# All four head pairs of a 256-token unit in one batch of array tiles per level, TensorE in program order, v through DRAM, first step of 512 tokens

## The chip, the cores and the metric

One core of one Trainium2 chip runs the kernel. The metric is device microseconds of that core, median of three runs. The profile is one further execution taken by the hardware profiler. Engines are named as in the profile: PE is TensorE's matmul, PEld its weight load, DVE VectorE, ACT ScalarE, POOL GpSimd, SP the queue that issues the DMAs.

## What is computed

A gated linear recurrence per head (batch 4, 8 heads, 768 tokens, head size 48), then a feed-forward layer on the 3072 tokens of width 8 x 48 = 384, inner width 2048, with a quick GELU:

```
f = 1 / (1 + exp(-f_logit))
state = 0
for t in range(S):
    state = f[:, :, t, :, None] * state + einsum('bhd,bhe->bhde', k[:, :, t], v[:, :, t])
    y[:, :, t] = einsum('bhd,bhde->bhe', q[:, :, t], state)
x = y.transpose(0, 2, 1, 3).reshape(B * S, H * D)
h = x @ w_in
out = (h * (1 / (1 + exp(-1.702 * h)))) @ w_out
```

All inputs are 32-bit floats but the two weight matrices, which arrive as 64-bit floats; the kernel turns their bits into 32-bit floats itself.

## The kernel before

**Units and pairs.** The 3072 tokens are 12 units of 256 tokens (`U`), three in each batch entry. A unit's heads are worked off as four pairs (`a`), two heads stacked on the 128 partitions, one in rows 0 to 47, the other in rows 64 to 111 (`rows`). `attention(n, a, ...)` does one pair: it turns f_logit, q and k with six transposes on TensorE (L187, L192), makes `F` (sigmoid, ACT, L188), `X` (q, q times f, k; L193, L194) and products of f over 2, 4, ... 64 tokens (`tot`, POOL, L203). In a chunk of 64 tokens the recurrence is replaced by six levels (`LEV` = 1, 2, 4, ... 32). At each level, tokens of the second halves meet keys of the first halves: four small matmuls give scores into `sc` (L217), one for each head and each group of 128 tokens (48 rows by 64 columns of the array each). Between two levels `promote` (L331, DVE) multiplies half of q and k in place by products of f, and ACT copies the keys of the next level to `Kc` (L235). DVE moves scores from PSUM to `A` under a mask, four slots of 64 at a time (L241). `add` multiplies `A` with rows of v (`vl`, seven arrangements of v, one for each level and half) into `py` (L256). Then k is turned back (L274, `kn`), gives the state increment of each chunk (`pd`, L281), the states follow each other in `st` (L293, L296), and q times f meets the state before its chunk in `py` (L306). ACT copies `py` to `yT` (L315), and ten DMAs in a unit (L320) carry it to `xT`, the input of the feed-forward layer, 0.5 us each to issue.

**Feed-forward.** `mlp_step` runs on a step: the first of unit 0 alone (256 tokens), five of two units (512 tokens) and the last of unit 11. It makes 16 blocks of h (three matmuls each, L342; sigmoid on ACT, L346; product on DVE, L347) and then, for each 128 tokens, 16 matmuls of 384 columns into `po` (L352). A 32-bit matmul shows as two instructions of each kind in the profile.

**Order.** The program text puts the attention of the next step between pieces of this step's feed-forward. The scheduler of the framework then orders every engine by itself; two lists of order edges (`issue_after`, L174) keep the matmuls on the banks of `py` apart. So on TensorE the bursts of small matmuls of one pair stand one by one between feed-forward matmuls.

**Loads.** `load_unit` issues six loads of raw q, k, f_logit, two of v by token (`vn`) and 28 of `vl`, whose pieces are single heads' rows of 48 floats. `raw`, `ld` and `att` tiles have two buffers, `sc`, `tr` and `y` in PSUM one. The weights (`load_weights`, L109) come in 28 pieces after unit 0, each with six DVE operations (L127 to L134) and one on POOL (L135).

## Time and profile before

| | us |
|---|---|
| median of three runs | 965.14 (960.77 to 965.42) |
| the profiled execution's own time | 966.6 |
| its span, first to last instruction | 964.9 |
| PE busy in it | 879.1 |

A row of the chain of waits gives a start and the time from there to the next piece of the chain, all in us; a row of a group gives total busy us and the mean ns of one. Busy time of PE is not work done, since ends of matmuls are modelled; how long a run of matmuls takes is read from when the next one starts. The granted clock (PEclk) has two levels, 1.2 GHz (0.50) and 2.4 GHz (1.00). No clock is recorded before 75 us, and the page shows 1.00 there.

### The profile page before, as it was taken

The page shows a single profiled execution, that of the slowest core. Times are in us where ns is not written, and L with a number is a line of the kernel's source. Part 1 is how long each engine was busy: PE and PEld are TensorE (multiplying, and loading weights), DVE is VectorE, ACT ScalarE, POOL GpSimd, SP SyncE. Part 2 cuts the span into 40 slices and gives each one's busy share as a digit, 9 for nine tenths or more (in the row PEclk, how much of TensorE's full clock was granted, in tenths as well). Part 3 has the DMA queues.
Part 4 walks back from the last instruction along what each step waited for, and adds up shares of the span by engine and source line. Part 5 has one row for each costly group of instructions (what it writes and reads, how often), then busy time and mean ns, then how long its engine had stood idle before and what let it go on. Part 6 is the DMA issues. An engine that isn't in the chain of part 4 may idle for free.

```text
span 964.9 us, 20905 instructions
## 1 busy us (share of the span) xinstructions
PE 879.1 (91%) x8672; PEld 473.7 (49%) x8672; DVE 385.3 (40%) x904; ACT 240.8 (25%) x617; POOL 126.0 (13%) x345
## 2 busy tenths in 40 slices
PE   2677888667799999999999999999999999999998
PEld 1444644343444555444555444555444554445584
DVE  1688866332344323344332444322444233331220
ACT  1212211222233222233222333222333222221120
POOL 5233323101001011010010100101001010000000
PEclk9997987655699999999999999999999999999999
DMA  7743363161442613314314315205206100000000
GB/s 113 180 133 102 113 161 98 44 99 22 65 67 42 99 33 70 71 29 55 64 42 69 69 21 81 59 20 110 39 12 108 35 26 14 5 5 13 22 9 16
DMA packets 205343, 58.78 MB, mean 61 GB/s; under 512 B 193985, under 2 KB 201665, under 8 KB 205249
## 3 DMA queue, kind: packets, MB, share of 16 engines
q1 hardware_dynamic: 205248, 57.45, 29.7%
q8 instruction: 68, 1.11, 0.5%
q14 instruction: 27, 0.21, 0.1%
HBM read 47.97 MB, written 4.72 MB: 55 GB/s over the span
## 4 chain that ended last, share of the span: by engine, by line
PE 83%; DVE 7%; SPq 3%; ACT 3%; POOL 2%; issue 2%; DMA 1%; DVEq 0%; ACTq 0%
PE o L352 28%; PE h L342 27%; PE sc L217 9%; PE y L256 7%; PE y L306 3%; PE tqk L192 3%; PE dS L281 2%; PE tk L274 2%; PE tf L187 2%; DVE X L331 2%; POOL w_out L135 1%; SPq L163 1%; DVE A L241 1%; DVE s L131 1%; DVE a L134 1%
## 5 line engine op out<-in xcount | busy, mean ns | idle before, releaser
L352 PE MATMUL o<-w_out,g 128*128 128x384 f32 x768 | 306.0, 517 | 8.7 <-POOL w_out L135 8.7
L342 PE MATMUL h<-xT,w_in 128*128 128x512 f32 (+1 forms) x672 | 307.7, 571 | 0.8 <-DMA xT<-yT 0.6
L352 PEld LDWEIGHTS o<-w_out,g 128*128 128x128 f32 x768 | 131.2, 193 | 67.4 <-POOL w_out L135 10.5
L331 DVE TENSOR_TENSOR X<-X,tot 128x256 f32<-128x256 f32 x240 | 105.1, 438 | 131.3 <-PE sc L217 130.9
L235 ACT COPY Kc<-X 128x128 f32<-128x128 f32 x240 | 71.8, 299 | 295.6 <-DVE X L331 295.6
L342 PEld LDWEIGHTS h<-xT,w_in 128*128 128x128 f32 x672 | 113.5, 194 | 38.2 <-issue 21.4
L217 PEld LDWEIGHTS sc<-X,Kc 48*64 48x64 f32 x1920 | 58.0, 143 | 142.8 <-ACT Kc L235 135.2
L217 PE MATMUL sc<-X,Kc 48*64 48x64 f32 x1920 | 93.0, 258 | 27.1 <-ACT Kc L235 26.9
L256 PEld LDWEIGHTS y<-A,vl 64*48 64x48 f32 x2688 | 70.6, 133 | 75.2 <-DVE A L241 45.6
L203 POOL TENSOR_TENSOR tot<-F 128x128 f32<-128x128 f32 x48 | 19.6, 409 | 665.7 <-ACT F L188 665.6
L256 PE MATMUL y<-A,vl 64*48 64x64 f32 (+1 forms) x2688 | 91.1, 251 | 14.6 <-DVE A L241 14.1
L347 DVE TENSOR_TENSOR g<-h,sg 128x512 f32<-128x512 f32 (+1 forms) x112 | 68.4, 612 | 86.4 <-ACT sg L346 86.4
L241 DVE TENSOR_TENSOR A<-sc,masks 128x512 f32<-128x512 f32 x96 | 66.4, 691 | 74.5 <-PE sc L217 74.5
L346 ACT ACTIVATE sg<-h 128x512 f32<-128x512 f32 (+1 forms) x112 | 60.0, 536 | 102.6 <-PE h L342 97.5
L296 DVE SCALAR_TENSOR_TENSOR st<-st,tot,dS 128x48 f32<-128x48 f32 x176 | 46.5, 264 | 66.6 <-PE dS L281 61.1
L194 DVE TENSOR_TENSOR X<-X,F 128x256 f32<-128x256 f32 x48 | 20.4, 425 | 122.5 <-ACT X L193 122.4
L203 POOL TENSOR_TENSOR tot<-tot 128x64 f32<-128x64 f32 (+4 forms) x240 | 63.4, 264 | 18.6
L315 ACT COPY yT<-y 48x256 f32<-48x256 f32 x96 | 35.1, 366 | 78.4 <-PE y L306 77.2
L306 PEld LDWEIGHTS y<-X,st 48*48 48x48 f32 x704 | 27.1, 130 | 39.8 <-DVE st L296 28.2
L276 ACT COPY kn<-tk 128x256 f32<-128x256 f32 x48 | 17.9, 372 | 105.7 <-PE tk L274 105.7
L217 PEld LDWEIGHTS sc<-X 48*64 48x64 f32 x768 | 24.2, 150 | 38.1 <-DVE X L194 37.6
L217 PE MATMUL sc<-X 48*64 48x128 f32 (+1 forms) x768 | 31.3, 282 | 12.1 <-DVE X L194 11.6
(33 smaller groups left out, 421.5 us busy)
## 6 DMA issues: line engine op xcount, KB each, us to landing
bits<-in_moe_w_in_dram SPq DMA_DIRECT2D x12, 512.0 KB, 3.5
bits<-in_moe_w_out_dram SPq DMA_DIRECT2D x16, 384.0 KB, 3.3
raw<-in_f_logit_dram SPq DMA_DIRECT2D x24, 192.0 KB, 3.2
raw<-in_q_dram SPq DMA_DIRECT2D x24, 192.0 KB, 4.6
raw<-in_k_dram SPq DMA_DIRECT2D x24, 192.0 KB, 5.0
vn<-in_v_dram SPq DMA_DIRECT2D x24, 192.0 KB, 3.1
vl<-in_v_dram SPq DMA_DIRECT2D x24, 192.0 KB, 3.3
vl<-in_v_dram SPq DMA_DIRECT2D x96, 48.0 KB, 2.4
```

Source lines behind the costliest of these rows:

```text
L203: nc.gpsimd.tensor_tensor(tn, t2[:, :, 0], t2[:, :, 1], ALU.mult)
L217: nc.tensor.matmul(sc[g * HS:(g + 1) * HS, h, slot * 64:slot * 64 + w], lhsT=lhs(h, g), rhs=rhs(h, g), start=True, stop=True,)
L235: nc.scalar.copy(Kc[:, l, :].rearrange("p (n m) -> p n m", m=LEV[l]), X[:, 2].rearrange("p (n two m) -> p n two m", two=2, m=LEV[l])[:, :, ...
L241: nc.vector.tensor_tensor(At, sc[:, :, :256].rearrange("p h (s t) -> p h s t", t=64), masks[r].unsqueeze(1).broadcast_to((P, 2, 4, 64)), A ...
L256: prior.append(nc.tensor.matmul(dst(h, g), lhsT=vl[g * 64:(g + 1) * 64, u, 2 * a + h, :], rhs=rhs(h, g), start=start, stop=False, skip_gro ...
L296: nc.vector.scalar_tensor_tensor(st[:, c, :], before, D64[:, c:c + 1], d, op0=ALU.mult, op1=ALU.add)
L306: mm = nc.tensor.matmul(py[rows(h), c // 2, c % 2 * C:(c % 2 + 1) * C], lhsT=before[rows(h)], rhs=X[rows(h), 1, c * C:(c + 1) * C], start= ...
L331: nc.vector.tensor_tensor(qk, qk, by, ALU.mult)
L342: nc.tensor.matmul(ph, lhsT=w_in[:, n, ff * P:(ff + 1) * P], rhs=xT[:, n, :T], start=(n == 0), stop=(n == NK - 1))
L346: nc.scalar.activation(sg, ph, AF.Sigmoid, scale=1.702)
L347: nc.vector.tensor_tensor(g[-1][:, ff % FG, :], ph, sg, ALU.mult)
L352: nc.tensor.matmul(po, lhsT=g[ff // FG][:, ff % FG, tt * P:(tt + 1) * P], rhs=w_out[:, ff, :], start=(ff == 0), stop=(ff == NFF - 1),)
```

## The change

TensorE keeps the order of the program text (`manual_schedule`); the other engines are still ordered by the scheduler. `attention(n, ...)` now makes a list of 16 parts for a whole unit, with all four pairs in each: six T parts (four transposes each, j = f, q, k by two pairs), a W part with the first scores of level 1, a W part with the rest of them, level 2 and the first `add`, four W parts for the levels 4 to 32 (scores of one level, `add` of the one before), two T parts that turn k back, a W part with the last `add` and the state increments, and a W part with q against the states and the way out. The matmuls are the same in number and shape. `F`, `X`, `tot`, `Kc`, `A` hold 1024 columns in place of 256, so each DVE, ACT and POOL operation of a level does four pairs at once; `promote` of a level is issued ahead of the move of its scores (`evacuate`). The state's one operation for a chunk and pair becomes two for a chunk.

`merge` puts feed-forward blocks (`mlp_h`: one h block, `mlp_o`: four matmuls of one output tile) behind the parts, 16 blocks to a unit, three shares for a W part and one for a T part: behind the 16 parts stand 1, 0, 1, 0, 1, 0, 2, 1, 2, 1, 2, 1, 1, 0, 2, 1 blocks. The steps are six of 512 tokens. Step 0's h blocks run in two halves of 256 tokens in units 1 and 2, its outputs in unit 3; then step s runs in units 2s + 2 and 2s + 3, and step 5 alone at the end.

v goes to a buffer in DRAM in token order by one DMA, and from there to `vl` in seven DMAs with rows of 1536 bytes and to `vn` in one, issued behind the fifteenth part of the unit before. `raw`, `ld` and `att` have one buffer, but `yT`, `st`, `A` and `Kc` keep two. The weights come in 56 smaller pieces in units 0 to 2, each with two ACT operations (Sign, Abs), four on DVE and two on POOL.

```diff
-    ld = ctx.enter_context(tc.tile_pool(name="ld", bufs=2))
-    att = ctx.enter_context(tc.tile_pool(name="att", bufs=2))
+    ld = ctx.enter_context(tc.tile_pool(name="ld", bufs=1))
+    att = ctx.enter_context(tc.tile_pool(name="att", bufs=1))
+    ctx.enter_context(tc.manual_schedule(engines={mybir.EngineType.PE}))
...
-    raws = [const.tile([P, 3, NG, H, HS], F32, name=f"raw{j}") for j in range(2)]
-    for t in raws:
-        nc.gpsimd.memset(t[:, :, :, :, D:], 0.0)
+    raw = const.tile([P, 3, NG, H, HS], F32, name="raw")
+    for j in range(3):
+        nc.vector.memset(raw[:, j, :, :, D:], 0.0)
...
+    v_toks = [tc.dram_tile([U, DM], F32, name=f"v_tok{j}") for j in range(2)]
+    WI, WO = 256, 192
...
-        bits = wp.tile([P, w, 2], I32, tag="bits", name=f"bits_{n}")
+        nc.sync.dma_start(out=bits.rearrange("p c two -> p (c two)"), in_=src.bitcast(I32))
...
-        a, s = tmp("a"), tmp("s")
-        ve.tensor_scalar(a, hi, 0x7FFFFFFF, None, op0=ALU.bitwise_and)
-        ve.tensor_scalar(s, hi, -(1 << 31), -(1 << 31), op0=ALU.bitwise_and, op1=ALU.bitwise_xor)
-        af = a.bitcast(F32)
-        ve.tensor_scalar(af, af, 2.0 ** 112, 2.0 ** 97, op0=ALU.mult, op1=ALU.max)
-        ve.scalar_tensor_tensor(s, a, 3, s, op0=ALU.logical_shift_left, op1=ALU.bitwise_xor)
-        ve.tensor_scalar(a, s, -(1 << 23), None, op0=ALU.bitwise_and)
-        ve.scalar_tensor_tensor(af, lo.bitcast(U32), 2.0 ** -52, af, op0=ALU.mult, op1=ALU.mult)
-        po.tensor_tensor(dst, s.bitcast(F32), af, ALU.add)
+        nc.scalar.activation(sign, hi.bitcast(F32), AF.Sign)
+        nc.scalar.activation(a, hi.bitcast(F32), AF.Abs, scale=2.0 ** 112)
+        ve.tensor_scalar(a, a, 2.0 ** 97, None, op0=ALU.max)
+        ve.tensor_scalar(
+            s.bitcast(I32), a.bitcast(I32), 3, -(1 << 31), op0=ALU.logical_shift_left, op1=ALU.bitwise_xor
+        )
+        ve.tensor_scalar(a.bitcast(I32), s.bitcast(I32), -(1 << 23), None, op0=ALU.bitwise_and)
+        ve.scalar_tensor_tensor(a, lo.bitcast(U32), 2.0 ** -52, a, op0=ALU.mult, op1=ALU.mult)
+        po.tensor_tensor(a, a, s, ALU.add)
+        po.tensor_tensor(dst, a, sign, ALU.mult)
...
-        for u, (m, half) in enumerate(V_HALF):
-            src = v[b, :, s0:s0 + U, :].rearrange("h (n two m) d -> two n m h d", two=2, m=m)[half]
-            nb = U // (2 * m)
-            if m <= nb:
-                for i in range(m):
-                    nc.sync.dma_start(out=vl[i:P:m, u], in_=src[:, i])
-            else:
-                for i in range(nb):
-                    nc.sync.dma_start(out=vl[i * m:(i + 1) * m, u], in_=src[i])
+    def load_v(n):
+        b, s0 = n // NU, n % NU * U
+        v_tok = v_toks[n % 2]
+        nc.sync.dma_start(
+            out=v_tok.rearrange("t (h d) -> t h d", h=H),
+            in_=v[b, :, s0:s0 + U, :].rearrange("h t d -> t h d"),
+        )
+        vl = ld.tile([P, NV, DM], F32, tag="vl", name=f"vl_{n}")
+        for u, (m, half) in enumerate(V_HALF):
+            nc.sync.dma_start(
+                out=vl[:, u], in_=v_tok.rearrange("(n two m) e -> two n m e", two=2, m=m)[half]
+            )
+        vn = ld.tile([P, NG, DM], F32, tag="vn", name=f"vn_{n}")
+        nc.sync.dma_start(out=vn, in_=v_tok.rearrange("(g p) e -> p g e", g=NG))
+        return vl, vn
...
+    TILES = [(h, g) for h in range(2) for g in range(NG)]
...
+            pt = ps.tile([P, 2, NG, P], F32, tag="tr", name=f"t{'fqk'[j]}_{n}_{a0}")
+            for a in range(2):
+                for g in range(NG):
+                    nc.tensor.transpose(
+                        pt[:, a, g, :], raw[:, j, g, 2 * (a0 + a):2 * (a0 + a + 1), :].rearrange("p h d -> p (h d)"), ident
+                    )
...
+            cols = slice(a0 * U, (a0 + 2) * U)
+            src = pt.rearrange("p a g t -> p (a g t)")
+            if j == 0:
+                nc.scalar.activation(t["F"][:, cols], src, AF.Sigmoid)
+            else:
+                nc.scalar.copy(t["X"][:, 2 * (j - 1), cols], src)
...
+            if j == 1:
+                nc.vector.tensor_tensor(t["X"][:, 1, cols], t["X"][:, 0, cols], t["F"][:, cols], ALU.mult)
...
+        for j in range(3):
+            for a0 in (0, 2):
+                part("T")(lambda j=j, a0=a0: turn(j, a0))
...
+        def score(out, lhs, rhs):
+            for a in range(NP):
+                for h, g in TILES:
+                    nc.tensor.matmul(
+                        out[g * HS:(g + 1) * HS, h, a, :], lhsT=lhs(h, a * U + g * G), rhs=rhs(h, a * U + g * G),
+                        start=True, stop=True,
+                    )
...
+        def evacuate(width, slots):
+            A = att.tile([P, 2, width], F32, tag=f"A{width}", name=f"A_{n}_{slots[0][1]}", bufs=2)
+            w = width // len(slots)
+            for c, l in slots:
+                nc.vector.tensor_tensor(
+                    A[:, :, c:c + w].rearrange("p h (x t) -> p h x t", t=64),
+                    t["sc"][:, :, c:c + w].rearrange("p h (x t) -> p h x t", t=64),
+                    masks[:, l, :].unsqueeze(1).unsqueeze(1).broadcast_to((P, 2, w // 64, 64)), ALU.mult,
+                )
+            return A
...
+            m = LEV[l]
+            nb = NA // (2 * m)
+            X = t["X"]
+            qk = view(X, NA + m, [[NA - m, 2], [2 * m, nb], [1, m]])
+            by = t["tms"][l].rearrange("p (n two) -> p two n", two=2).unsqueeze(3).broadcast_to((P, 2, nb, m))
+            nc.vector.tensor_tensor(qk, qk, by, ALU.mult)
+            if l + 1 < NL:
+                m = LEV[l + 1]
+                Kc = t["Kc"] = att.tile([P, NA // 2], F32, tag="Kc", name=f"Kc_{n}_{l}", bufs=2)
+                nc.scalar.copy(
+                    Kc.rearrange("p (n m) -> p n m", m=m),
+                    X[:, 2].rearrange("p (n two m) -> p n two m", two=2, m=m)[:, :, 0, :],
...
+        def add(u, A, dst, start=False):
+            for a in range(NP):
+                for h, g in TILES:
+                    nc.tensor.matmul(
+                        dst(h, g, a), lhsT=t["vl"][g * 64:(g + 1) * 64, u, (2 * a + h) * D:(2 * a + h + 1) * D],
+                        rhs=A(h, g, a), start=(start and a == 0), stop=False, skip_group_check=True,
+                    )
...
+        @part("W")
+        def _():
+            t["vl"], t["vn"] = loaded()
+            sc = scores()
+            score(
+                sc.rearrange("p h (a t) -> p h a t", a=NP), lambda h, x: t["X"][rows(h), 2, x:x + G:2],
+                lambda h, x: view(t["X"], x, [[NA + 1, 2], [2, 64]])[rows(h)],
+            )
+            promote(0)
+            t["A"] = evacuate(512, [(0, 0)])
+        @part("W")
+        def _():
+            sc = scores()
+            s4 = sc.rearrange("p h (s a t) -> p s h a t", s=2, a=NP)
+            score(s4[:, 0], lambda h, x: t["X"][rows(h), 2, x + 1:x + G:2], lambda h, x: t["X"][rows(h), 0, x + 1:x + G:2])
+            score(s4[:, 1], keys(1), tokens(1, LEV[1], 1))
+            A = t["A"]
+            t["py"] = ps.tile([P, NG, NP, G], F32, tag="y", name=f"y_{n}")
+            add(
+                0, lambda h, g, a: A[g * 64:(g + 1) * 64, h, a * G:(a + 1) * G].rearrange("p (two n) -> p n two", two=2),
+                lambda h, g, a: t["py"][rows(h), g, a, :], start=True,
+            )
+            promote(1)
+            t["A"] = evacuate(512, [(0, 0), (256, 1)])
+        def level(l):
+            sc = scores()
+            score(sc[:, :, :256].rearrange("p h (a t) -> p h a t", a=NP), keys(l), tokens(1, LEV[l], 1))
+            if l == 2:
+                add(1, slot(t["A"], 0), half(1, 1))
+                add(2, slot(t["A"], 256), half(LEV[1], 1))
+            else:
+                add(l, slot(t["A"], 0), half(LEV[l - 1], 1))
+            promote(l)
+            t["A"] = evacuate(256, [(0, l)])
+        for l in range(2, NL):
+            part("W")(lambda l=l: level(l))
...
+        @part("W")
+        def _():
+            add(NL, slot(t["A"], 0), half(LEV[-1], 1))
+            pd = scores()
+            for a in range(NP):
+                for g in range(NG):
+                    for h in range(2):
+                        for c in range(2):
+                            x = (a * NG + g) * D
+                            nc.tensor.matmul(
+                                pd[h * HS:(h + 1) * HS, c, x:x + D],
+                                lhsT=t["kn"][c * C:(c + 1) * C, a, g, h * HS:(h + 1) * HS],
+                                rhs=t["vn"][c * C:(c + 1) * C, g, (2 * a + h) * D:(2 * a + h + 1) * D],
+                                start=True, stop=True,
...
+            py = t["py"]
+            for c in [1, 2, 3, 0][:NC - first]:
+                for a in range(NP):
+                    for h in range(2):
+                        x = a * U + c * C
+                        nc.tensor.matmul(
+                            py[rows(h), c // 2, a, c % 2 * C:(c % 2 + 1) * C], lhsT=t["before"][c][rows(h), a],
+                            rhs=t["X"][rows(h), 1, x:x + C], start=False, stop=True, skip_group_check=True,
+                        )
+            yT = att.tile([P, NP, NG, G], F32, tag="yT", name=f"yT_{n}", bufs=2)
+            for h in range(2):
+                nc.scalar.copy(yT[rows(h)].rearrange("p a g t -> p g a t"), py[rows(h)])
+                for a in range(NP):
+                    f0, f1 = (2 * a + h) * D, (2 * a + h + 1) * D
+                    while f0 < f1:
+                        end = min(f1, (f0 // P + 1) * P)
+                        r0 = h * HS + f0 - (2 * a + h) * D
+                        nc.sync.dma_start(
+                            out=xT[f0 % P:f0 % P + end - f0, f0 // P, x0:x0 + U],
+                            in_=yT[r0:r0 + end - f0, a].rearrange("p g t -> p (g t)"),
+                        )
+                        f0 = end
...
+    def mlp_h(g, s, xT, t0, t1):
+        def block(ff):
+            if ff % FG == 0 and t0 == 0:
+                g.append(mlp.tile([P, FG, TM], F32, tag="g", name=f"g_{s}_{ff}", bufs=5))
+            T = t1 - t0
+            ph = ps.tile([P, TM], F32, tag="mm", name=f"h_{s}_{ff}_{t0}", bufs=3)
+            for n in range(NK):
+                nc.tensor.matmul(
+                    ph[:, :T], lhsT=w_in[:, n, ff * P:(ff + 1) * P], rhs=xT[:, n, t0:t1],
+                    start=(n == 0), stop=(n == NK - 1),
...
+    def mlp_o(g, s):
+        def some(tt, ff0):
+            for ff in range(ff0, ff0 + 4):
+                nc.tensor.matmul(
+                    po, lhsT=g[ff // FG][:, ff % FG, tt * P:(tt + 1) * P], rhs=w_out[:, ff, :],
+                    start=(ff == 0), stop=(ff == NFF - 1),
+                )
...
+    def merge(parts, fill, share):
+        total = sum(share(kind, i) for i, (kind, _) in enumerate(parts))
+        at = done = 0
+        for i, (kind, fn) in enumerate(parts):
+            fn()
+            at += share(kind, i)
+            while done < len(fill) * at / total:
+                fill[done]()
+                done += 1
+    def even(kind, i):
+        return 3 if kind == "W" else 1
...
+    def unit(n):
+        if n % 2 == 0:
+            xTs[n // 2] = mlp.tile([P, NK, TM], F32, tag="xT", name=f"xT_{n // 2}")
+        parts = attention(n, lambda: loads[n], xTs[n // 2], n % 2 * U)
+        def then(i, load):
+            kind, fn = parts[i]
+            parts[i] = (kind, lambda: (fn(), load(n + 1)))
+        if n + 1 < NALL:
+            then(5, load_raw)
+            then(14, load)
+        return parts
...
+    load_raw(0)
+    load(0)
+    merge(unit(0), weights[:NI], lambda kind, i: 1)
+    g = {s: [] for s in range(NALL // 2)}
+    u1 = unit(1)
+    merge(u1[:8], weights[NI:NI + 8], lambda kind, i: 1)
+    merge(u1[8:], weights[NI + 8:NI + 16] + mlp_h(g[0], 0, xTs[0], 0, U), lambda kind, i: 1)
+    merge(unit(2), [f for p in zip(mlp_h(g[0], 0, xTs[0], U, TM), weights[NI + 16:]) for f in p], even)
+    merge(unit(3), mlp_o(g[0], 0), even)
+    for s in range(1, NALL // 2):
+        fill = mlp_h(g[s], s, xTs[s], 0, TM) + mlp_o(g[s], s)
+        if s + 1 == NALL // 2:
+            for f in fill:
+                f()
+            continue
+        for j in range(2):
+            merge(unit(2 * (s + 1) + j), fill[j * len(fill) // 2:(j + 1) * len(fill) // 2], even)
```

## Rows read from the trace of the kernel before

**Rows 1.** Windows: us, then each engine's busy us (instructions), granted clock, DMA share, GB/s.

```profile
395.80:812.50 416.70, 416.36 (x4301) 210.14 (x4303) 156.47 (x361) 118.64 (x301) 41.92 (x149) 1.00 0.28 51
```

**Rows 2.** Chain of waits, 622 to 638 us: start, us to the next piece, what.

```profile
623.37 1.49 PE o L352 x4
...
628.29 0.28 PE sc L217 x8
...
631.81 0.59 PE y L256 x32
...
633.42 0.38 PE dS L281 x16
...
634.65 0.36 PE y L306 x8
...
637.86 0.44 PE tqk L192 x4
```

**Rows 3.** Chain of waits, whole span: runs of feed-forward matmuls.

```profile
430.31 1.72 PE h L342 x4
...
920.03 20.72 PE h L342 x96
940.75 20.65 PE o L352 x64
```

**Rows 4.** Groups by line and form: busy us, mean ns of one; idle before.

```profile
L331 DVE TENSOR_TENSOR X<-X,tot 128x256 f32<-128x256 f32 x240 | 105.1, 438 | 131.3 <-PE sc L217 130.9
...
L235 ACT COPY Kc<-X 128x128 f32<-128x128 f32 x240 | 71.8, 299 | 295.6 <-DVE X L331 295.6
...
L241 DVE TENSOR_TENSOR A<-sc,masks 128x512 f32<-128x512 f32 x96 | 66.4, 691 | 74.5 <-PE sc L217 74.5
...
L193 ACT COPY X<-tqk 128x512 f32<-128x512 f32 x48 | 28.1, 585 | 34.3 <-PE tqk L192 34.1
...
L135 POOL TENSOR_TENSOR w_in<-s,a 128x512 f32<-128x512 f32 x12 | 15.6, 1298 | 39.7 <-DVE a L134 39.7
...
L134 DVE SCALAR_TENSOR_TENSOR a<-bits,a 128x512 f32<-128x512 uint32 x12 | 8.2, 685 | 0.1
...
L133 DVE TENSOR_SCALAR a<-s 128x512 int32<-128x512 int32 x12 | 5.1, 424 | 0.3
...
L188 ACT ACT_TABLE_LOAD x1 | 1.3, 1283 | 0.8 <-PEq L416 0.8
```

**Rows 5.** SP's timeline: a unit's last xT DMAs.

```profile
566.23 1.82 SPq L320 DMA_DIRECT2D xT<-yT  x3
```

**Rows 6.** PE's timeline at the start: start, modelled us, what, idle before.

```profile
11.34 0.69 PE L187 MATMUL tf<-ident,raw 128*128 128x128 f32 x2 [11.34 <-POOL raw L99]
12.50 1.11 PE L192 MATMUL tqk<-ident,raw 128*128 128x128 f32 x4 [0.47 <-ACT F L188]
...
19.89 0.49 PE L217 MATMUL sc<-X,Kc 48*64 48x64 f32 x8 [0.55 <-ACT Kc L235]
21.36 0.49 PE L217 MATMUL sc<-X,Kc 48*64 48x64 f32 x8 [0.97 <-ACT Kc L235]
...
41.92 1.11 PE L256 MATMUL y<-A,vl 64*48 64x64 f32 x32 [0.81 <-DVE A L241]
```

**Rows 7.** Windows, as in Rows 1, where the clock fell, and after.

```profile
115.00:120.00 5.00, 2.62 (x8) 1.21 (x6) 3.52 (x10) 0.00 (x0) 1.25 (x2) 0.90 0.52 138
120.00:125.00 5.00, 5.00 (x10) 2.42 (x9) 3.70 (x9) 0.00 (x0) 0.99 (x1) 0.50 0.81 209
...
130.00:135.00 5.00, 4.06 (x48) 1.87 (x47) 4.04 (x11) 0.84 (x3) 1.10 (x1) 1.00 0.64 123
```

**Rows 8.** DMA issues by line: count, KB each, median us to landing.

```profile
raw<-in_f_logit_dram SPq DMA_DIRECT2D x24, 192.0 KB, 3.2
...
vl<-in_v_dram SPq DMA_DIRECT2D x24, 192.0 KB, 3.3
...
xT<-yT SPq DMA_DIRECT2D x72, 48.0 KB, 1.9
```

More of the change, by code (lines that the diff above doesn't have):

```diff
@@ L1 @@
 from contextlib import ExitStack
+from itertools import count
 import concourse.bass as bass
@@ L217, in score, with _ @@
+            last["st"] = st
+        @part("W")
+        def _():
+            py = t["py"]
[3 more added lines that the diff above has]
+                        x = a * U + c * C
                         nc.tensor.matmul(
[L218 to L224 removed]
@@ new lines, with load @@
+    xTs, loads = {}, {}
+    def unit(n):
[8 more added lines that the diff above has]
+            then(14, load)
+        return parts
+    def load(n):
+        loads[n] = load_v(n)
```

280 lines of the change are left out of this document (82 added, 198 removed).

## The prediction

> **What bounds the kernel now.** First the windows: from 395.8 to 812.5 us PE is busy for 416.4 of 416.7 us at the full clock, DVE for 156 and ACT for 119 [rows 1]. So TensorE sets the time there, and only what it does in fewer microseconds counts. Then the chain of waits inside that stretch, for what a piece of PE's time consists of [rows 2], and its runs of feed-forward matmuls alone, for their own price [rows 3]. 64 output matmul instructions take 20.65 us, 0.323 each; the h instructions take 0.43 with 512 columns and 0.216 with 256 [rows 3]. There are 768, 480 and 192 of them, so the feed-forward is 247.8 + 206.4 + 41.4 = 495.6 us, 82.6 for a step of 512 tokens, 2.58 for one of the 32 blocks that such a step has. The stretch holds three steps of 138.9 us, each with eight pairs: (138.9 - 82.6) / 8 = 7.04 us of TensorE for a pair.
>
> Most of the 7.04 isn't arithmetic. A burst of 8 small instructions takes 0.28 us, one of 32 takes 0.59 [rows 2]: 0.013 for each more, 0.052 for four (four array tiles side by side), and 0.18 that every burst costs once. The four output instructions behind a burst take 1.49 us [rows 2] and not 4 x 0.323 = 1.29: another 0.20. A round trip to array tiles and back therefore costs 0.38 us, whatever is in it, and a pair makes about ten: 3.8 us. The rest is 3.1 us (below), together 6.9 against the 7.04 measured.
>
> **The batch.** The matmuls stay the same in number and shape. In one unit the scores and `add` are 128 groups of four at 64 columns (a matmul of 128 columns counted as two): 128 x 0.052 = 6.6 us. The state increments, 0.38 - 0.18 for 16 instructions, are 0.8 for 64; q against the states, 0.36 - 0.18 for 8, is 1.45 for 64; 32 transposes at 0.11 are 3.5 [rows 2]. Sum 12.4 us. There are eight W parts and T parts are in the mode of the feed-forward, so eight round trips: 3.0. TensorE needs 15.4 us for a unit where four pairs need 28.2.
>
> **Program order.** TensorE now stands still where an operand is late, and all feed-forward blocks are queued behind the waiting matmul. I go through the parts. Promoting 256 columns takes 0.438 and 512 columns of the same kind 0.691 [rows 4], so 1024 take 1.2. From one level's scores to the next: a feed-forward product of 512 columns that DVE may have ahead (0.69), promote (1.2), the move of the scores out of the only `sc` buffer (0.69), handoffs 0.24 (a level at the start takes 21.36 - 19.89 = 1.47, which is the burst's 0.49, 0.438, 0.299 for `Kc`, and that [rows 4, 6]): 2.8 us. `Kc` (0.585 by the 512-column copy [rows 4]) runs beside the move. Cover is the `add` (0.41), 0.20 and at least one block (2.58): 3.2. For the second W part it is 3.5 against 3.6. So the levels are hidden, with little to spare: without the block's cover each would cost about 2.6. Its bounds are 0 and 1 us for each of the 96 W parts; I take 0.1, 8 us in all, because the start's level shows no delay beyond its operations.
>
> T parts: behind the second, fourth and sixth stands no block, and `tr` has one buffer. The next part waits for 0.18 + 0.585 [rows 4] + two handoffs, 0.9 us; three times, and 0.45 for `kn`, whose other half an `add` covers: 3.2 us. A unit with 16 blocks then lasts 41.3 + 15.4 + 3.2 = 59.9 us.
>
> **Step boundary.** One block and one T part, 3.2 us, stand between a unit's last y matmul and the first h block that reads its `xT`. In that time ACT copies 1024 columns twice (0.97 each, by 0.299 for 128 and 0.585 for 512 [rows 4]) and SP issues ten DMAs, three of which take 1.82 [rows 5]. The first third of `xT` needs the sixth: 1.2 + 6 x 0.61 + 1.9 to land [rows 8] = 6.8 us. The wait is 3.6, and 0.7 more for the last third: 4.3. A stretch in which TensorE was idle for half of 5 us was followed by 5 us at the lower level, 0.50 [rows 7], which loses 2.5. I take 6 us for each of five boundaries, 30, between 4 and 10 each. Queued behind are h blocks and the next T parts; ACT, DVE and POOL only wait with them.
>
> **v through DRAM.** No row has a DRAM to DRAM copy. A load of half its size in the same 192-byte pieces lands in 3.3 us [rows 8]: at least 3.3, at most two of those and eight more in series behind it, 33; nearest is the row itself, so 15 with the eight reads overlapping. The reads wait for the copy and for the last `add` of the unit before (`vl` has one buffer). From there to the next unit's first `add` lie two W parts, six T parts and eight blocks, about 29 us: nothing on the path, 4 us for a unit if at its end. SP's issues fall from 36 to 15 loads a unit. In unit 0 the need comes at about 23 us, so up to 10 is possible there.
>
> **The start.** The first transpose waits until 11.34 for POOL's clearing of `raw` [rows 6]. This clearing is now DVE's, and the loads land in 3.2 [rows 8], so I start at 5. TensorE is at the half clock there: a burst of 32 takes 1.11 [rows 6] against 0.59. Unit 0 has no blocks and runs along the chain: six T parts at 1.11 + 0.59 + 0.16 = 1.8 [rows 4, 6], 11; the first W parts 4.7 and 4.8 (scores 1.9, promote 1.2, moves 1.2 to 1.4, handoffs); four levels at 1.1 + 2.1 = 3.3, 13; turning k 3.6; increments and states 4; y 3. It ends at 49. Beside it DVE converts 24 pieces: three operations of about 0.29 and one of 0.43 at 256 columns (by 0.424 and 0.685 at 512 [rows 4]), 1.3 each, 31 us, with 17 of its own (six promotes 7.2, moves 5.4, two products 1.4, states about 2.7): 48 in 44 us. So DVE binds, and I take 60, between 49 and 80. POOL has two sums of about 0.7 for a piece (1.298 at 512 [rows 4]), 34 us, which fits. Unit 1: 20 us to its second W part, 7 for two levels, and 35 for 16 h blocks of 256 columns (20.7 us at the full clock, 41 at half) with the rest: 62. Unit 2: TensorE 15.4 + 20.7 = 36, DVE 42 with 16 pieces, latencies between: 52. Unit 3 is a full unit: 60. Together 234, between 205 and 270.
>
> **The sum.** 234 + 8 x 59.9 + 30 + 82.6 for the last step + 8 + 3.5 (the last copy and store, as now: 964.9 less 940.75 + 20.65 [rows 3]) = 837 us of span. The profiled execution's time is 1.7 above its span and 1.5 above the median of the runs, so the span stands for the median; I say 840. Against now: three steps of the middle cost 138.9 each, then 82.6 + 37.2 + 6 = 126.
>
> **Rivals.** (1) The start stays cold: units 0 to 2 at the half clock with DVE late throughout. Their 174 becomes 220: 885. For it speaks that TensorE is idle between parts there. (2) Everything hides, the start at 205, boundaries 4: 798. (3) The scores' tiles now take turns in `h` outside `g`, so two neighbours share rows of the array; all bursts in the trace alternate rows. If such tiles went one after the other, scores (half of the 6.6) would double: 3.3 x 12 = 40, 880. Against it: y against the states runs two tiles side by side at the same pace. (4) ACT has to reload its table between Sigmoid and Sign or Abs, which no row shows; copies need no reload, since the trace has one load, of 1.28 us [rows 4]. Two for each of 56 pieces are 143 us on ACT, beside some 80 of its own in the 174 us of units 0 to 2: 50 more, 890. (5) **Slower:** the clock falls in every unit. The T phase is about 13 us with 3 of waiting, in single microseconds. If TensorE stayed at the half level through it and the levels behind it, over 20 us of a unit's 60, each unit would pay 10 or more; from 10.5 us for each of twelve units the gain of 125 is gone, and with 25 us cold it is 12.5 x 12, 990. For it: the fall behind the half-idle stretch. Against it: from 130 us TensorE waited for a fifth of 5 us and kept the full level [rows 7]. The Trainium skill's page "TensorE: Matmul & The Clock Gate", section "Loop structure matters more than you think", wants matmuls back to back and has the clock drop at waits between bursts; it speaks against program order, and one fall in this trace agrees with it.
>
> **How the numbers follow.** The forecast (800 to 870) has 0.62, rival 1 0.15, 2 0.08, 3 0.04, 4 0.04, 5 0.07. Eight times in ten: 795 to 888. A change of 0.5% (5 us) is about what a measurement of this kernel can tell; faster by more 0.92, within 0.01, slower by more 0.07.
>
> **What would show it.** Right: bursts of 32 and 64 small instructions, eight to a unit; steps of some 126 us; a gap of 4 to 6 us ahead of each step's first h block, put down to `xT`; gaps under 1 us behind every other T part. Wrong: scores waiting for `A` or `Kc` at each level, a burst of 32 scores near 1 us at the full clock, `add` waiting for `vl`, more table loads on ACT, or a granted clock below 1.00 behind unit 3 other than at boundaries.

## The result, and the profile after

The changed kernel takes 873.85 us (median of four runs, 870.49 to 877.09) where the kernel before takes 965.28 on the same chip: a ratio of 0.906, 95% interval 0.901 to 0.911. It is faster, by 9.4%. The forecast was 840 with a range of 795 to 888, so the sign and the range held, and the size was 34 us too good.

The profiled execution took 871.83 us with a span of 870.1. Its page, first the engines, then PE and the granted clock in 40 slices of 21.8 us, then the chain that ended last:

```profile
PE 745.9 (86%) x8672; PEld 460.9 (53%) x8672; DVE 345.8 (40%) x611; ACT 223.6 (26%) x429; POOL 126.3 (15%) x204
...
PE   2445367899996999996999996999997999989998
...
PEclk9855559799998999998999997999999999999999
...
PE 71%; POOL 8%; issue 8%; ACT 4%; DMA 4%; SPq 4%; DVE 1%; POOLq 0%; ACTq 0%; DVEq 0%
```

PE is busy for 745.9 us where it was busy for 879.1, with the same matmuls: 133 us less, of which 38 are given back as idle time (124 us in place of 86) and 95 are the shorter span. From slice 9 on PE is full but for a dent every six slices (6, 6, 6, 7, 8): the boundaries of the steps. The first seven slices, some 150 us, are at 2 to 7 tenths with the clock at half for four of them, and POOL has 8% of the chain. No clock is recorded in this trace before 32 us, and the page shows 1.00 there; 32 scores at 28.79 us take 1.13, the duration of the half level.

The steady part, from the chain of waits (start, us to the next piece, what):

```profile
338.33 0.45 PE tf L199 x4
...
338.81 0.60 ACT F L205
...
339.46 0.66 PE tq L199 x4
...
354.21 1.12 PE sc L228 x64
...
356.43 2.78 PE o L429 x8
359.20 0.62 PE sc L228 x32
...
399.63 1.95 DMA xT<-yT
...
401.67 5.46 PE h L412 x6
...
409.16 2.59 PE h L412 x6
```

These answer [rows 2]. A burst has 32 or 64 small instructions where it had 4 to 32, and 32 scores take 0.62 us where 8 took 0.28. The block behind a burst takes 2.78 where a plain one takes 2.58: the 0.20 of the way back, now paid some eight times a unit. Between the scores of two levels PE waits for nothing here. It waits behind a T part (338.78 to 339.46, 0.68 us, for `F`) and at the boundary, where the h block comes 6 us late, at the half clock: 5.46 us for what takes 2.59 at 409.16.

How the span divides, by the first h block of step 1 and of step 5 in the timelines: 273.2 us of start (forecast 234 and the wait of a boundary, 238), 508.7 for four steps (127.2 each; the forecast's 126 leaves out the 0.8 us a unit that its sum has for late levels, with which it is 127.4), 88.2 for the end (forecast 86). The ends of units 0 to 3 stand at 72, 153.7, 206.2 and 265.6 us, and the windows between them are (us, busy us of PE, PEld, DVE, ACT, POOL, then granted clock, DMA share, GB/s; the 0.75 of the first counts the unrecorded 32 us as 1.00):

```profile
0.00:72.00 72.00, 29.24 (x592) 23.87 (x592) 50.28 (x105) 24.37 (x56) 41.17 (x65) 0.75 0.79 175
72.00:153.70 81.70, 48.46 (x691) 38.67 (x687) 62.48 (x161) 32.20 (x88) 47.81 (x70) 0.67 0.50 126
153.70:206.20 52.50, 47.83 (x725) 38.48 (x724) 30.84 (x61) 20.59 (x45) 9.08 (x17) 0.89 0.33 77
206.20:265.60 59.40, 57.99 (x721) 37.16 (x720) 16.69 (x23) 12.25 (x20) 3.13 (x6) 1.00 0.38 83
```

The forecast gave 60, 62, 52 and 60. Units 2 and 3 took that to within 0.6 us; units 0 and 1 took 12 and 20 us more, 32 of the 33 us by which the span exceeds the 837 of the sum. In them DVE is busy for 70% and 76% of the time: much, but it is not the bound that the forecast took it for.

### The profile page after: what moved, and what is told of

It reads as the page before. It is cut to its first block, busy times and chain, and to the rows that moved or that the text cites. A ratio compares the mean times of both kernels' runs of the same rounds, so it can differ in the third digit from the quotient of the medians.

```text
span 870.1 us, 19829 instructions
## 1 busy us (share of the span) xinstructions
PE 745.9 (86%) x8672; PEld 460.9 (53%) x8672; DVE 345.8 (40%) x611; ACT 223.6 (26%) x429; POOL 126.3 (15%) x204
## 4 chain that ended last, share of the span: by engine, by line
PE 71%; POOL 8%; issue 8%; ACT 4%; DMA 4%; SPq 4%; DVE 1%; POOLq 0%; ACTq 0%; DVEq 0%
PE h L412 28%; PE o L429 27%; PE sc L228 5%; PE y L277 4%; POOL a L140 4%; POOL w_out L141 2%; PE y L382 2%; SPq L394 2%; POOL w_in L141 2%; DMA vn<-v_tok 1%; DMA xT<-yT 1%; ACT X L207 1%; PE tq L199 1%; SPq L167 1%; PE tk L199 1%
## 5 line engine op out<-in xcount | busy, mean ns | idle before, releaser
L412 PE MATMUL h<-xT,w_in 128*128 128x512 f32 (+1 forms) x672 | 282.7, 569 | 31.0 <-DMA xT<-yT 25.7
L429 PE MATMUL o<-w_out,g 128*128 128x384 f32 x768 | 261.9, 491 | 0.0
L264 DVE TENSOR_TENSOR X<-X,tot 128x1024 f32<-128x1024 f32 x60 | 73.2, 1220 | 89.9 <-PE sc L228 89.8
L228 PE MATMUL sc<-X,Kc 48*64 48x64 f32 x1920 | 45.6, 238 | 34.4 <-DVE A L248 34.1
L268 ACT COPY Kc<-X 128x512 f32<-128x512 f32 x60 | 37.7, 628 | 132.9 <-DVE X L264 132.9
L228 PEld LDWEIGHTS sc<-X,Kc 48*64 48x64 f32 x1920 | 37.8, 148 | 61.1 <-issue 27.4
L277 PE MATMUL y<-A,vl 64*48 64x64 f32 (+1 forms) x2688 | 65.4, 243 | 0.0
L248 DVE TENSOR_TENSOR A<-sc,masks 128x512 f32<-128x512 f32 (+1 forms) x84 | 62.9, 759 | 0.0
L140 POOL TENSOR_TENSOR a<-a,s 128x192 f32<-128x192 f32 (+1 forms) x56 | 41.1, 734 | 60.5 <-DVE a L139 58.9
L388 ACT COPY yT<-y 48x1024 f32<-48x1024 f32 x24 | 24.2, 1006 | 47.7 <-PE y L382 47.4
L133 DVE TENSOR_SCALAR a<-a 128x192 f32<-128x192 f32 (+1 forms) x56 | 21.6, 387 | 37.1 <-ACT a L132 36.5
L228 PE MATMUL sc<-X 48*64 48x128 f32 (+1 forms) x768 | 27.2, 274 | 9.8 <-DVE A L248 9.1
L382 PE MATMUL y<-X,st 48*48 48x64 f32 x704 | 25.1, 228 | 9.0 <-DVE st L369 6.9
```

What stands on the lines that cost most here:

```text
L140: po.tensor_tensor(a, a, s, ALU.add)
L228: nc.tensor.matmul(out[g * HS:(g + 1) * HS, h, a, :], lhsT=lhs(h, a * U + g * G), rhs=rhs(h, a * U + g * G), start=True, stop=True,)
L248: nc.vector.tensor_tensor(A[:, :, c:c + w].rearrange("p h (x t) -> p h x t", t=64), t["sc"][:, :, c:c + w].rearrange("p h (x t) -> p h x t ...
L264: nc.vector.tensor_tensor(qk, qk, by, ALU.mult)
L268: nc.scalar.copy(Kc.rearrange("p (n m) -> p n m", m=m), X[:, 2].rearrange("p (n two m) -> p n two m", two=2, m=m)[:, :, 0, :],)
L277: nc.tensor.matmul(dst(h, g, a), lhsT=t["vl"][g * 64:(g + 1) * 64, u, (2 * a + h) * D:(2 * a + h + 1) * D], rhs=A(h, g, a), start=(start a ...
```

## Experiments: the start

The two theories for the 32 us. A: the conversion of the weights, which DVE, ACT and POOL make beside the attention of units 0 and 1, delays the chain more than its DVE time says. B: TensorE at the half clock and the latencies of a unit without cover. Within A, A1: POOL's part, by slowing DVE and by being waited for; A2: the number of DVE operations.

**The conversion as one copy on ACT.**

```diff
-        sign, a, s = tmp("sign"), tmp("a"), tmp("s")
...
-        po.tensor_tensor(dst, a, sign, ALU.mult)
+        nc.scalar.copy(dst, hi.bitcast(F32))
```

> The changed kernel with the weights' bit conversion left out: one ACT copy of the upper words stands in for its two ACT, four DVE and two POOL operations, so the output is not the reference's; pieces, loads and their places stay. Theory A (the conversion, beside the attention of units 0 and 1, is the excess over the predicted start): unit 1's way out moves from 154 us to about 115, unit 3 ends near 230 instead of 266, time 873.9 - 35 = about 838. Rival B (half clock and bare latency of the level chain make the start long; DVE's conversion sits in their gaps): unit 3's end stays within 10 us of 266, time 862 to 874.

Measured: 830.68 us, ratio 0.862 (0.859 to 0.866). Units 0 to 3 end at 55, 114, 166 and 224 by their last matmul, where by the same mark the changed kernel's end at 72, 154, 205 and 263. So A: the conversion costs the start some 40 us here, 5 more than expected, and without it the units come close to the durations of the forecast or below (55, 59, 52, 58). The clock does not carry it: PE's timeline of this kernel shows bursts in the first 36 us of unit 1 at the half-clock duration (1.1 us for 32 instructions, as [rows 6], against 0.59 in [rows 2]), and yet the unit takes 59 us in place of 82 (L216 here is L228 of the changed kernel):

```profile
73.32 1.10 PE L216 MATMUL sc<-X,Kc 48*64 48x64 f32 x32
...
77.12 1.14 PE L216 MATMUL sc<-X,Kc 48*64 48x64 f32 x32 [0.99 <-DVE A L236]
...
80.77 1.14 PE L216 MATMUL sc<-X,Kc 48*64 48x64 f32 x32 [0.81 <-ACT Kc L256]
```

One level follows the other after 3.7 to 3.8 us here. In PE's timeline of the changed kernel the same step of unit 1 takes 9.3, the longest of the unit; the next three take 6.5, 8.1 and 7.7, the last of them with one h block:

```profile
90.40 1.10 PE L228 MATMUL sc<-X,Kc 48*64 48x64 f32 x32
...
99.66 1.14 PE L228 MATMUL sc<-X,Kc 48*64 48x64 f32 x32 [6.46 <-DVE A L248]
```

The timeline of all engines in that stretch shows where it goes:

```profile
92.40 0.59 POOL L140 TENSOR_TENSOR a<-a,s 128x192 f32<-128x192 f32 x1 [1.79 <-DVE a L139]
...
94.28 0.59 POOL L141 TENSOR_TENSOR w_out<-a,sign 128x192 f32<-128x192 f32 x1
94.43 0.56 DVE L133 TENSOR_SCALAR a<-a 128x192 f32<-128x192 f32 x1 [1.23 <-ACT a L132]
...
95.65 0.26 DVE L133 TENSOR_SCALAR a<-a 128x192 f32<-128x192 f32 x1
...
96.26 1.68 POOL L140 TENSOR_TENSOR a<-a,s 128x192 f32<-128x192 f32 x1 [1.38 <-DVE a L139]
96.27 1.22 DVE L264 TENSOR_TENSOR X<-X,tot 128x1024 f32<-128x1024 f32 x1
...
97.40 0.65 DVE L138 TENSOR_SCALAR a<-s 128x192 int32<-128x192 int32 x1
```

Two things are to be seen. The promotion (L264) could start behind the scores at 91.5, but stands in DVE's queue behind operations of the conversion, one of which (94.43) waits 1.23 us for ACT. And DVE and POOL hold each other up: L133 takes 0.56 us while POOL works and 0.26 at 95.65 while it does not; POOL's sum takes 1.68 beside the promotion and 0.59 at 92.40 without it; L138 behind that takes 0.65, to 0.11 past POOL's end. Why ACT was late is in the table of waits (total us, times, longest):

```profile
PE sc L228 <- DVE A L248: 43.1, 10, 6.7
DVE a L133 <- ACT a L132: 36.5, 28, 11.6
ACT sign L131 <- POOL w_out L141: 34.5, 24, 3.4
...
ACT sign L131 <- POOL w_in L141: 27.1, 17, 2.9
```

ACT's Sign for a piece waits for POOL to finish with the buffer of a piece before, 41 times, 62 us in all; DVE waits for ACT; the scores wait for DVE. POOL's 41 us in unit 0 (the forecast had 34) fit into its 72, as the forecast had it; its place in a ring of three engines with few buffers did not.

**POOL's two operations taken out** (a copy on ACT in their place):

```diff
-        po.tensor_tensor(a, a, s, ALU.add)
-        po.tensor_tensor(dst, a, sign, ALU.mult)
+        nc.scalar.copy(dst, a)
```

> The changed kernel with the two ACT and four DVE operations of the conversion, but an ACT copy in place of POOL's sum and product, so the weights' values are not the reference's. Theory A1 (POOL is the cause: DVE operations of 256 columns take 0.29 us alone and 0.55 beside POOL, and ACT and DVE wait for POOL's buffers): most of the gain of leaving out all of it, 840 to 850, DVE's mean of the three single-input operations back at 0.29. Theory A2 (DVE's count of operations ahead of promote in its queue is the cause, whatever POOL does): 860 to 870.

Measured: 842.75 us, ratio 0.876 (0.873 to 0.880); units end at 62, 127, 181, 239. The same four DVE operations as in the changed kernel stay, and 29 us of the 42 go (0.906 less 0.876, by 962): A1. In its windows unit 1 has the clock of the changed kernel, 0.68 against 0.67, and takes 17 us less, which speaks against B once more:

```profile
62.00:127.00 65.00, 43.39 (x695) 35.92 (x690) 49.11 (x160) 42.21 (x119) 3.20 (x6) 0.68 0.62 159
```

The groups by form, mean ns before the last bar, of the changed kernel for pieces of 192 columns:

```profile
L139 DVE SCALAR_TENSOR_TENSOR a<-bits,a 128x192 f32<-128x192 uint32 x32 | 13.2, 416 | 0.3
L134 DVE TENSOR_SCALAR s<-a 128x192 int32<-128x192 int32 x32 | 12.8, 402 | 0.6
...
L138 DVE TENSOR_SCALAR a<-s 128x192 int32<-128x192 int32 x32 | 11.1, 350 | 0.6
L133 DVE TENSOR_SCALAR a<-a 128x192 f32<-128x192 f32 x32 | 11.1, 346 | 16.4 <-ACT a L132 16.2
```

and of the kernel without POOL:

```profile
L139 DVE SCALAR_TENSOR_TENSOR a<-bits,a 128x192 f32<-128x192 uint32 x32 | 11.2, 356 | 0.4
...
L133 DVE TENSOR_SCALAR a<-a 128x192 f32<-128x192 f32 x32 | 8.2, 258 | 9.5 <-ACT a L132 9.4
L138 DVE TENSOR_SCALAR a<-s 128x192 int32<-128x192 int32 x32 | 8.1, 258 | 0.4
L134 DVE TENSOR_SCALAR s<-a 128x192 int32<-128x192 int32 x32 | 8.1, 257 | 0.4
```

A piece costs DVE 1.51 us beside POOL and 1.13 without it. The remaining 13 us up to the first experiment would be the DVE work itself and ACT's queue; no run parts these.

**A third buffer, and the conversion of the kernel before.** One leaves the operations and loosens the ring; the other has six DVE operations and one of POOL for a piece and nothing on ACT:

```diff
-            return wp.tile([P, w], F32, tag=tag, name=f"{tag}_{n}")
+            return wp.tile([P, w], F32, tag=tag, name=f"{tag}_{n}", bufs=3)
```

> The changed kernel with three buffers in place of two for the conversion's intermediate tiles. If ACT waiting for POOL to release them (61 us of ACT's waits) is what reaches the attention through DVE's queue: unit 1 ends 10 us sooner, time about 863. If it is DVE's slower operations or their number: no change, 870 to 876.

```diff
-        nc.scalar.activation(sign, hi.bitcast(F32), AF.Sign)
-        nc.scalar.activation(a, hi.bitcast(F32), AF.Abs, scale=2.0 ** 112)
+        ve.tensor_scalar(a, hi, 0x7FFFFFFF, None, op0=ALU.bitwise_and)
+        ve.tensor_scalar(s, hi, -(1 << 31), -(1 << 31), op0=ALU.bitwise_and, op1=ALU.bitwise_xor)
...
-        po.tensor_tensor(a, a, s, ALU.add)
-        po.tensor_tensor(dst, a, sign, ALU.mult)
+        po.tensor_tensor(dst, s.bitcast(F32), af, ALU.add)
```

> The changed kernel with the earlier conversion: six DVE operations and one POOL sum for a piece, no ACT operation; piece sizes 256 and 192 columns as in the changed kernel. DVE has 36 us more work without POOL beside it (103 in place of 67), POOL half. If the cause is POOL's share and the link from ACT to DVE (A1): not slower, 860 to 874. If the cause is DVE's work (A2): slower, 890 or more.

Measured: 866.93 us (ratio 0.900, 0.897 to 0.904) and 858.95 (0.892, 0.889 to 0.895). The buffer gives some 6 us, between the two expectations, and the two intervals touch (0.901 to 0.911 for the change). ACT still waits 41 us for POOL with it (32 times) where it waited 62, so this run loosens the ring without taking it away, and how large the ring's part is stays open. The earlier conversion is 13 us faster than the new one although it gives DVE two more operations a piece: against A2, and it says that this part of the change costs time. How A1's 29 us divide between slower DVE operations and waiting for POOL is not settled by these runs.

## Experiments: the boundaries, the order and v

**Where the boundary's wait comes from.** SP's queue at the boundary of 401.67 us:

```profile
384.32 4.51 SPq L167 DMA_DIRECT2D vl<-v_tok  x7
388.94 0.41 SPq L171 DMA_DIRECT2D vn<-v_tok  x1
394.92 0.62 SPq L160 DMA_DIRECT2D v_tok<-in_v_dram  x1
395.60 7.16 SPq L394 DMA_DIRECT2D xT<-yT  x10
```

The ten issues of `xT` take 7.16 us [rows 5 show 1.82 for three], and the first stands behind the copy of a later unit's v (394.92), which waits until `vn` has been read out of one of the two `v_tok` buffers. Over the whole run such copies wait 26 us for reads of `vn`, by the table of waits of SP's queue:

```profile
SPq L160 <- DMA vn<-v_tok: 26.1, 8, 5.4
```

Three kernels take one thing each: a buffer for every unit's v; three output blocks kept back and put behind the boundary's T parts; and equal shares, which put one block behind every part but so leave less in front of the boundary.

```diff
-    v_toks = [tc.dram_tile([U, DM], F32, name=f"v_tok{j}") for j in range(2)]
+    v_toks = [tc.dram_tile([U, DM], F32, name=f"v_tok{j}") for j in range(NALL)]
...
-        v_tok = v_toks[n % 2]
+        v_tok = v_toks[n]
```

> The changed kernel with one DRAM buffer of v for each unit in place of two, so the copy of v for a later unit no longer waits for the reads of an earlier one. Theory: at a step's end the SP queue holds that waiting copy in front of the ten xT DMAs (first xT DMA 2 us behind its ACT copy); without it the gap ahead of each step's first h block falls from 6 to 7 us to 4 to 5, with the clock's fall shorter: 860 to 866. Rival: the gap is ACT's copies and SP's ten issues alone: no change, 870 to 876.

```diff
-    merge(unit(3), mlp_o(g[0], 0), even)
+    LATE = 3
+    late = mlp_o(g[0], 0)
+    merge(unit(3), late[:-LATE], even)
+    late = late[-LATE:]
...
-        fill = mlp_h(g[s], s, xTs[s], 0, TM) + mlp_o(g[s], s)
+        fill = late + mlp_h(g[s], s, xTs[s], 0, TM) + mlp_o(g[s], s)
...
+        fill, late = fill[:-LATE], fill[-LATE:]
```

> The changed kernel with the last three output blocks of every step moved behind the first T parts of the next step's unit, ahead of its first h block. Theory (boundary): 7.7 us more cover the way of xT, the gaps of 3.2 to 7.0 us ahead of the five first h blocks and the half clock behind them go: 5 x 7 = 35 us, about 838. Rival: the wait moves with the blocks (next unit's g or mm buffers, or DMAs queued later): gain under 12 us, 862 to 874.

```diff
-        return 3 if kind == "W" else 1
+        return 1
```

> The changed kernel with one feed-forward block behind every part of the units from 2 on (shares 1 and 1 in place of 3 and 1). Theory: a T part then has a block in front of the next part's use of the one tr buffer; the two waits of 0.69 us in a unit and the 0.45 us by which the first score burst is stretched go, 1.8 us for each of nine or ten units, and one block still covers a level (2.8 of 3.2 us): about 857. Rival: one block doesn't cover a level behind every W part; scores then wait for A, up to 1 us for each of eight parts, and the time is 874 or more.

Measured:

| | us, ratio to before | start | four steps | end |
|---|---|---|---|---|
| the change | 873.85, 0.906 (0.901 to 0.911) | 273.2 | 508.7 | 88.2 |
| v ahead | 855.12, 0.891 (0.887 to 0.894) | 263.0 | 499.8 | 89.4 |
| blocks shifted | 832.70, 0.867 (0.864 to 0.869) | 271.7 | 473.0 | 86.3 |
| equal shares | 857.61, 0.893 (0.890 to 0.895) | 270.0 | 496.3 | 87.7 |

With blocks shifted the first h block of a step stands behind T parts, so the start holds more there and the last of the four steps less: they take 120.0, 119.5, 119.4 and 114.1 us.

With v ahead the gaps at the five boundaries are 3.0 to 3.6 us where they were 7.0, 6.0, 7.0, 3.2 and 3.6: the two shorter ones had no such copy in front, and the other three now look like them. The start is 10.2 us shorter, which puts the time below what was expected: 3.9 of it are the gap of the first boundary, and unit 1 takes 74.5 us where it took 81.5. What made the wait there is not shown. With blocks shifted the chain runs over all five boundaries without a gap and at the full clock; the one behind unit 5:

```profile
386.70 0.66 PE tk L199 x4
387.35 2.60 PE o L429 x8
...
391.05 0.69 PE sc L228 x16
391.74 5.35 PE h L412 x12
```

Twelve h instructions in 5.35 us here, six in 5.46 in the change. The span is 39.1 us shorter over five boundaries: 7.8 each, of which the gaps are 5.3 (26.7 / 5). The rest, 12.4 in all, fits the clock: the h blocks right behind the five gaps take 2.5, 2.9, 2.9, 1.7 and 2.0 us more in the change than at the full level. Equal shares give 12.4 us in four steps, although the first four boundary gaps grow to 9.8, 8.7, 7.7 and 5.0: the waits behind T parts are gone.

**Program order and the batch apart.** One kernel is the change without the line that fixes TensorE's order, the other is the kernel before with that line:

```diff
-    ctx.enter_context(tc.manual_schedule(engines={mybir.EngineType.PE}))
```

> The changed kernel without the fixed order on TensorE: the scheduler orders it as in the kernel before. It tells the batch from the program order. Theory: nearly all of the gain is the batch (eight round trips to array tiles a unit in place of forty); a scheduler that splits the batches again loses part of it: 860 to 920, and the number of bursts in a unit tells how much. Rival: program order carries the gain, so without it the time is near 950 or more.

```diff
+    ctx.enter_context(tc.manual_schedule(engines={mybir.EngineType.PE}))
```

> The kernel before with program order on TensorE alone, without the batch. A pair's own chain (turns, six levels, states) then stands in the order of the text with nothing between, and its four feed-forward blocks behind it. Theory: program order is a cost that only large parts with blocks between them can carry; a pair alone lasts 14 us or so in place of 7, so 44 x 7 = 300 us more, 1150 to 1300. Rival: TensorE's queue reaches far enough to cover it: under 1000.

Measured: 832.34 us, ratio 0.866 (0.864 to 0.869), for the change in free order, and 1428.64 in a single run for the kernel before in program order. Both left what was expected of them. In free order the start is 256.3, the four steps 485.5, the end 87.8: all of it faster. The bursts stay together (93 of them in the trace; 86 in the change, 419 in the kernel before), so the batch does not need the fixed order. The scheduler covers waits that the hand-made shares leave open: the gaps of the first four boundaries are 3.1, 3.0, 3.7 and 0.4 us. It also shortens unit 1 to 60 us, with the same conversion, part of which it moves into unit 2 (DVE has 121 and 101 operations in these two units where it had 161 and 61), and unit 3 ends at 247 in place of 263. This suggests that what the conversion costs the start hangs on where its operations stand among those of the attention, and not on their number alone. The kernel before cannot bear program order at all. Its chain between two levels of one pair:

```profile
801.67 0.44 DVE X L333
...
802.13 0.31 ACT Kc L237
...
802.48 0.54 PE sc L219 x8
```

One level in 1.47 us, 0.49 of it TensorE's by its timeline, with nothing beside it; a pair then takes 28.7 us (229.8 for a step of eight) where it takes 17.4 [rows 1: 138.9 / 8], and the granted clock is at half for some 655 of the 1427 us. So program order gives nothing here; it costs the changed kernel some 38 us (0.906 less 0.866, by 962). The Trainium skill's page "TensorE: Matmul & The Clock Gate", section "Loop structure matters more than you think", has TensorE run cold where a long wait, in its example one for a DMA, stands before each of its matmuls. In this trace the waits are short ones for other engines, 0.97 us of each 1.47, and the clock fell too, for the 655 us.

**v straight from its input,** two loads for `vn` and 28 for `vl` as before, all else as in the change:

```diff
-        v_tok = v_toks[n % 2]
...
+            if m <= nb:
+                for i in range(m):
+                    nc.sync.dma_start(out=vl[i:P:m, u].rearrange("p (h d) -> p h d", h=H), in_=src[:, i])
```

> The changed kernel with v loaded straight into vl and vn in single heads' rows by 30 DMAs, as in the kernel before, in place of the copy in DRAM and eight DMAs. Theory: vl has one buffer, so all 30 issues of some 0.5 us come between the last add and the xT DMAs; the SP queue then holds xT up by about 8 us at every step: 900 to 920. Rival 1: the scheduler puts the xT DMAs first or the issues hide: 860 to 876. Rival 2: the copy's waits cost more than the issues: faster than 860.

Measured: 924.84 us, ratio 0.961 (0.957 to 0.965), a little over what was expected: with one `vl` buffer and program order, the way through DRAM is worth 53 us. Without the new way of v the change gains 38 us in place of 91. SP's timeline at the same boundary:

```profile
409.78 2.07 SPq L170 DMA_DIRECT2D vl<-in_v_dram  x2
...
413.37 10.32 SPq L170 DMA_DIRECT2D vl<-in_v_dram  x14
423.73 5.85 SPq L173 DMA_DIRECT2D vl<-in_v_dram  x12
429.68 6.28 SPq L397 DMA_DIRECT2D xT<-yT  x10
```

Thirty issues stand ahead of `xT`, 20 us of queue, and four of the boundary gaps are 12.9 to 13.8 us. The start is 25 us longer, the four steps 26.

**All that helped, in one kernel,** in program order and in free order: the earlier conversion with a third buffer, equal shares, v ahead, three blocks shifted.

> The changed kernel with five of the changes together: the earlier conversion (alone 15 us), three buffers for it, one block behind every part (16), a DRAM buffer for each unit (of its 19 us some 7 at the start, the rest at boundaries), and three output blocks behind the boundary (41). If the causes are separate: 874 - 41 - 16 - 15 - 7 = 795, within 8. If they overlap (the start is one bound whichever part is mended): 808 to 820.

> The same without the fixed order on TensorE. Theory: program order costs only what waits in order, and those waits are mended here, so freeing the order brings little: within 1% of the kernel with the order, 790 to 803. Rival: the free order still gains as it did alone (40 us): 765 or less; or it splits batches again: more bursts and slower by 10 or more.

Measured: 802.87 us, ratio 0.833 (0.830 to 0.837), and 799.89, 0.831 (0.828 to 0.834), the lowest medians here; the two are not apart beyond their intervals. The first lies at the upper end of what was expected if the causes add up (787 to 803), so most of them do. Two steps of the first in windows, columns as above:

```profile
256.30:371.90 115.60, 115.60 (x1442) 68.65 (x1441) 42.49 (x61) 30.25 (x51) 6.11 (x12) 1.00 0.30 70
371.90:487.10 115.20, 115.20 (x1427) 68.25 (x1426) 42.76 (x62) 30.30 (x51) 5.64 (x12) 1.00 0.26 66
```

TensorE has no gap left and the full clock, and the first three steps of both kernels take the same 115.2 to 115.6 us, the last 113.8. So in the steps the order is indifferent once every wait has a block in front of it. What is left over is the start: unit 3 ends at 247 and 244 us, where in the kernel with the one copy on ACT it ends at 224.

## Why the forecast was right and where it was wrong

**The batch: right.** The round trip at 0.38 us carried the forecast, and its parts stand in the chain after: 0.20 behind a burst (2.78 less 2.58) and bursts that grow by their instructions alone. A unit's TensorE time without any wait is (115.2 - 82.6) / 2 = 16.3 us where 15.4 were summed and 28.2 were paid. In free order, with nothing but the batch changed on TensorE, the kernel is faster still. The batch with v straight from its input still gains, 0.961, but 53 of the 91 us are gone, since its 30 issues then hold up `xT`. No run has the new way of v in the kernel before; that it would not have helped in the middle is argued from [rows 1], where TensorE was never idle.

**Waits in program order: right in sum.** With blocks shifted, a step without boundary takes 119.5 us, 18.45 a unit beside feed-forward; the forecast had 15.4 + 3.2 + 0.8 = 19.4. Within that, the levels wait for nothing (0.8 forecast), the T parts show two gaps of 0.68 us and a first burst of scores stretched by its operand, and TensorE's own part is 0.9 higher. (0.1 us for each of 96 W parts is 9.6; the sum's 8 is 0.8 for each of ten units.) That the steps came out at 127.2 us against 127.4 is in part luck: the boundary took 1.8 us more than the sum has, and two units 1.9 less.

**The boundary: right in kind, 7.8 us in place of 6.** The gap stands ahead of each step's first h block, is put down to `xT`, and is followed by the half clock, as said. What the sum left out is the copy of v in front of `xT` on SP's queue; with v ahead the gaps are 3.0 to 3.6 us, below the 4.3 of the sum.

**v through DRAM: right for its readers, wrong for the queue.** "Nothing on the path" was worked out for the readers of v, and TensorE shows no wait for `vl` or `vn`. The price came from the other side of the queue: an issue that waits for a buffer holds the issues behind it, 2.8 to 4.0 us at three boundaries. That the forecast names 4 us for a copy at a unit's end is luck, since that is the copy's own time and not a wait in front of `xT`. Left out too was what the shorter queue gives: with 30 issues a boundary's gap is 13 us.

**The start: the step that failed.** Forecast 234 us to the end of unit 3, measured 265.6. "DVE binds" at 1.3 us a piece and "POOL fits" were both sums over one engine. Measured are 1.82 us (256 columns) and 1.51 (192) for a piece on DVE, against 1.40 and 1.13 with POOL silent, and the forecast's 1.3 for 256 columns, from [rows 4], is near the 1.40 with POOL silent. And the conversion is a ring of ACT, DVE and POOL whose waits stood in DVE's queue ahead of the promotions: unit 1, for which no DVE bound was made at all, took 82 us in place of 62, with DVE busy for 62 of them. Program order seems to have a share in this: in free order, with the same conversion, unit 3 ends 16 us sooner.

**The rivals.** Rival 1 is half right: units 0 to 2 took 206 us where the sum has 174 and the rival 220, and DVE was late, as it says. The half clock is not what it costs: with it for the first 36 us and no conversion unit 1 takes 59 us. Rival 2 is false: the start took 266 us and not 205, a boundary 7.8 and not 4. Rival 3 is false: 32 scores in 0.62 us and 64 in 1.12 keep the pace of the other bursts. Rival 4 is false: one table load in the trace. Rival 5 is false here, since behind unit 3 the clock falls at boundaries alone; the kernel before in program order shows that its mechanism exists, where a level has no cover.

## What to carry to other kernels

Small matmuls on array tiles paid 0.38 us here for each round trip into the mode and back, more than a burst of eight takes in all (0.28), so count the trips as well as the instructions, and put independent problems into one burst. When TensorE's order is fixed by hand, every wait needs a block of its own in front of it and every transfer's issue must not stand behind one that waits; try the scheduler's order beside it, as it may do better until the cover is complete. Work that several engines share in a chain is not costed by the busiest engine: follow the ring of buffers and the order in each engine's queue, and take durations from stretches where the same engines work side by side.

## What the runs showed of the hardware

DVE and POOL don't slow each other a little; the rows look like one waiting for the other. DVE's promotion from 96.27 to 97.49 lies beside a POOL sum that takes 1.68 us in place of 0.59, and a DVE operation of 0.25 us that starts at 97.40 ends 0.11 us after that sum. Over all pieces the DVE operations with one input rise from 0.26 to 0.35 to 0.40 us. The Trainium skill's page "SBUF — State Buffer", section "SBUF: two separate sides", says that the two engines share a pair of ports as an exclusive lock (of VectorE's operations those in a two-port mode or with two inputs in SBUF take it), and that the one that comes second is blocked until the first has finished. The rows agree.

One copy that waits in SP's queue cost three boundaries up to 4 us each. And a mean granted clock does not tell a stretch's time where TensorE waits for others: at 0.67 and 0.68 unit 1 took 82 us and 65, by what the other engines had to do.
